# Unit 2's attention in two query chunks, with the first MoE product of batch 0 begun beside the second chunk

## The chip, the cores and the metric

One core of a Trainium2 chip runs the whole kernel. The metric is the time on the device, in microseconds (us), as the median of several runs. A core has five engines that run their own instruction streams, each in program order, and wait for each other through semaphores: TensorE (PE: matrix products into the accumulators in PSUM), VectorE (DVE), ScalarE (ACT: exponentials and other functions), GpSimd (POOL) and SyncE (SP, which issues transfers). DMA engines move data between the memory of the chip and the core's own memory.

## The reference

```python
def _attn_ref(q, k, v, g_q, g_k):                      # q, k, v: (8, 12, 448, 64)
    def rmsnorm(x, g):
        rms = np.sqrt(np.mean(x * x, axis=-1, keepdims=True) + 1e-06)
        return x / rms * g
    q_n, k_n = (rmsnorm(q, g_q), rmsnorm(k, g_k))
    scores = scale * np.matmul(q_n, k_n.transpose(0, 1, 3, 2))
    scores = scores - np.max(scores, axis=-1, keepdims=True)
    attn = np.exp(scores)
    attn = attn / (np.sum(attn, axis=-1, keepdims=True) + 1e-09)
    return np.matmul(attn, v).astype(np.float32)

def _moe_ref(x, w_in, w_out):                          # x: (3584, 768)
    h = x @ w_in                                       # w_in: (768, 2048)
    g = np.maximum(0.01 * h, h)
    return (g @ w_out).astype(np.float32)              # w_out: (2048, 768)
```

Attention with normalised queries and keys, and behind it two products with a leaky ReLU between them. A token of the second part is one position of one batch, and its 768 features are the 12 heads, so the first product of a batch needs the attention of all its heads, for those tokens that it is to compute.

## The kernel before

The work is cut into 24 **units** of four heads; three units make a batch. A unit's path is:

1. load the queries and keys (DMA), square them (ACT or POOL), sum the squares (DVE), form 1/rms by a logarithm and an exponential (ACT, `prep_rinv`), multiply (DVE, `prep_norm`), transpose (PE, `prep_tr`) and copy out of PSUM (DVE or ACT);
2. scores of the first of seven key tiles, their maximum over everything (DVE, `shift_max`), which a product with a matrix of ones spreads to all partitions (`shift_mm`); this is what the exponentials subtract, one number for the whole unit;
3. for each of the seven key tiles the scores (PE, `qk`) and their exponential (ACT, `ex`);
4. the row sums (PE, `zsum`), their reciprocal by logarithm and exponential (ACT, `zinv`), the product with the values (PE, `pv`), and that times the reciprocal (DVE, `xmul`), which gives `xt`, the input of the first MoE product.

The 448 positions of a head lie as seven groups of 64. PSUM has eight banks: two slots of two banks (`slot()`) and four single banks (`aux()`), which come from a pool or, after `hold()`, from a list that `drop()` fills.

```python
    def aux(shape, dtype, name):
        if held:
            return held[0].pop(0)
        return psum.tile(shape, dtype, tag="aux", bufs=4, name=name)

    def hold():
        if not held:
            banks = [psum.tile([P, 512], FP32, tag="aux", bufs=4, name=f"bank{i}") for i in range(4)]
            held.append(banks)

    def drop(bank):
        if held:
            held[0].append(bank)
    ...
    def prep_rinv(u, tis=BOTH):
        x = slice(tis[0], tis[-1] + 1)
        nc.scalar.activation(buf(u, "uu")[:, x], buf(u, "ssq")[:, x], AF.Ln, bias=eps_t, scale=1.0 / D)
        nc.scalar.activation(buf(u, "rinv")[:, x], buf(u, "uu")[:, x], AF.Exp, bias=0.0, scale=-0.5)
    ...
    def prep_tr(u, ti, copies):
        tp = aux([P, NS, P], FP16, "tp")
        for (lo, hi), copy in copies:
            for x in range(lo, hi):
                nc.tensor.transpose(tp[:, x, :], buf(u, "n16")[:, ti, x].rearrange("p a d -> p (a d)"), ident16)
            copy(buf(u, "qkT")[:, ti, lo:hi], tp[:, lo:hi], ti == 0)
    ...
    def slot():
        return psum.tile([P, 2, 512], FP32, tag="sT", bufs=2, name="sT")
    ...
    def score(u, t, banks):
        for r in range(2):
            for a in range(2):
                nc.tensor.matmul(banks[a][64 * r:64 * r + 64, 0:S].rearrange("p (t x) -> p t x", t=NS),
                                 kT(u, r, a, t), qT(u, r, a), start=True, stop=True)
    ...
    def ex(u):
        s = st[u]
        ...
        for t, sT in s["sT"]:
            if isinstance(sT, list):
                for a in range(2):
                    nc.scalar.activation(s["et"][:, t, a], sT[a][:, 0:S], AF.Exp, bias=s["eb"], scale=1.0)
            else:
                nc.scalar.activation(s["et"][:, t], sT[:, :, 0:S], AF.Exp, bias=s["eb"], scale=1.0)

    def score0(u):
        banks = [aux([P, 512], FP32, "s0") for a in range(2)]
        score(u, 0, banks)
        st[u]["sT"] = [(0, banks)]

    def shift_max(u):
        s = st[u]
        sT = s["sT"][0][1]
        if isinstance(sT, list):
            pm2 = small.tile([P, 2], FP32, tag="pm2", name="pm2")
            for a in range(2):
                nc.vector.tensor_reduce(pm2[:, a:a + 1], sT[a][:, 0:S], axis=AXL.X, op=ALU.max)
            s["spare"] = sT[0]
            nc.vector.tensor_reduce(s["spare"][:, 511:512], pm2, axis=AXL.X, op=ALU.max)
        else:
            s["spare"] = sT[:, 0]
            nc.vector.tensor_reduce(s["spare"][:, 511:512], sT[:, :, 0:S], axis=AXL.XY, op=ALU.max)
        s["dg"] = small.tile([P, P], FP16, tag="dg", name="dg")
        nc.vector.tensor_tensor(s["dg"], ident16, s["spare"][:, 511:512].broadcast_to([P, P]), op=ALU.mult)
    ...
    def zsum(u, t0=0, t1=NS):
        s = st[u]
        for t in range(t0, t1):
            for r in range(2):
                for a in range(2):
                    nc.tensor.matmul(s["zt"][r][64 * a:64 * a + 64, 0:S], ones16[64 * r:64 * r + 64],
                                     s["et"][64 * r:64 * r + 64, t, a], start=(t == 0), stop=(t == NS - 1))
    ...
    def pv(u, t0=0, t1=NS):
        s = st[u]
        if t0 == 0 and "pslot" not in s:
            s["pv"] = [aux([P, 512], FP32, "pv") for r in range(2)]
        for t in range(t0, t1):
            for r in range(2):
                for a in range(2):
                    nc.tensor.matmul(s["pv"][r][64 * a:64 * a + 64, 0:S], vts[u % NV][64 * r:64 * r + 64, a, t],
                                     s["et"][64 * r:64 * r + 64, t, a], start=(t == 0), stop=(t == NS - 1))

    def xmul(u):
        s = st[u]
        b, g = divmod(u, NQ)
        if b not in xts:
            xts[b] = xpool.tile([P, NQ, 2, S], FP16, tag="xt", name="xt")
        for r in range(2):
            nc.vector.tensor_tensor(xts[b][:, g, r], s["pv"][r][:, 0:S], s["rz"][:, r], op=ALU.mult)
            drop(s["pv"][r])

    def prelu(b, dst, src):
        if b % 2 == 0:
            src = src.rearrange("p (t x) -> p t x", t=NS)[:, ::-1]
            dst = dst.rearrange("p (t x) -> p t x", t=NS)
        nc.scalar.activation(dst, src, AF.Prelu, bias=0.0, scale=1.0, alpha=0.01)

    def moe1(b, ft):
        xt = xts[b]
        hps = aux([P, 512], FP32, "hps")
        for kt in range(KT):
            nc.tensor.matmul(hps[:, 0:S], win16[:, kt // 2, kt % 2, ts(ft, P)], xt[:, kt // 2, kt % 2],
                             start=(kt == 0), stop=(kt == KT - 1))
        prelu(b, gt[:, ft, 64 * (b % 2):64 * (b % 2) + S], hps[:, 0:S])
        drop(hps)
```

`moe1` is one of 16 tiles of the first MoE product of a batch: six matmuls over all 448 tokens, and a leaky ReLU on ACT into `gt`; `moe1_part` does some of the six matmuls of the first two tiles, and `sums` is `zsum` and `pv` for some key tiles. `zinv` stands in the diff below. MoE items stand in a queue, and from unit 3 on `fill` puts some of them between the steps of the attention, so many that the queue lasts until the next batch is finished. The order in which everything is issued is fixed by the program. From the middle of unit 1 on, and the start of the loop (the part before it is in the diff):

```python
        trn(2, 1, vcopy)
        xmul(0)
        qk(1, (4,))
        ex(1)
        qk(1, (5,))
        ex(1)
        score0(2)
        shift_max(2)
        qk(1, (6,))
        ex(1)
        shift_bank(2)
        warm(12, st[2]["pb"])
        shift_mm(2)
        prep_ssq(3)
        ex(2)
        qk(2, (1,))
        ex(2)
        zsum_slot(1)
        pv(1)
        prep_rinv(3)
        zinv(1)

        prep_norm(3)
        ...
        qk(2, (2,))
        ex(2)
        trn(3, 0, vcopy)
        trn(3, 1, vcopy)
        xmul(1)
        prep_ssq(4)
        qk(2, (3,))
        ex(2)
        qk(2, (4,))
        ex(2)
        st[2]["zt"] = [aux([P, 512], FP32, "zt") for r in range(2)]
        sums(2, 0, 3)
        qk(2, (5,))
        ex(2)
        sums(2, 3, 4)
        qk(2, (6,))
        ex(2)
        prep_rinv(4)
        sums(2, 4, 5)
        qk(3, STEPS[0])
        sums(2, 5, NS)
        zinv(2)
        shift_max(3)
        xmul(2)
        push(0)
        first = slot()
        moe1_part(0, first, 0, KT - 2)
        shift_mm(3)
        ex(3)
        moe1_part(0, first, KT - 2, KT - 1)
        moe1_part(0, first, KT - 1, KT)
        for ft in range(2):
            prelu(0, gt[:, ft, 0:S], first[:, ft, 0:S])
        del queue[0:2]

        for u in range(3, NU):
            for d in range(4):
                if d > 0 or u > 3:
                    qk(u, STEPS[d])
                    if d == 0:
                        shift_max(u)
                        if u == 6:
                            xmul_sb(u - 2)
                        if narrow(u - 1):
                            pv_slot(u - 1)
                            zcol(u - 1)
                            shift_mm(u)
                            pv_out(u - 1)
                        else:
                            zsum_slot(u - 1)
                            pv(u - 1)
                            shift_mm(u)
                            zinv(u - 1)
                    ex(u)
                ...
                if d == 0:
                    if u == 3:
                        prep_norm(4)
                        gate(4)
                    ...
                if (u, d) in ((3, 1), (4, 0)):
                    for ti in range(2):
                        prep_tr(u + 1, ti, VV)
                ...
                fill(u, d, jobs)
```

`warm` issues products that nobody reads.

## Time and profile before

| what | value |
|---|---|
| median of three runs | 421.74 us (421.12 to 422.13) |
| span of the profiled execution | 420.3 us |
| PE busy | 404.4 us (96%), 3959 matmuls |
| ACT busy | 303.6 us (72%) |
| DVE busy | 269.2 us (64%) |
| POOL busy | 83.0 us (20%) |
| moved by DMA | 62.42 MB |

The page of the profile gives the busy time of each engine, then the span in 40 slices of 10.5 us, each a digit for the busy share in tenths. Matmuls are pipelined, so a busy PE is not PE at its peak. The timeline lists instructions by time, with like ones merged: start, duration, engine, line of the program, operation, what is written and read, the shapes, the count, and in brackets how long the engine stood idle before and what ended that. The table by stages gives busy times for stretches of the span. The chain of waits follows the last instruction back through what released each step.

### The profile page before, as it was taken

How to read it: one execution, taken by the hardware profiler on the slowest of the kernel's cores; microseconds unless marked ns; L12 is line 12 of the kernel's file. 1: busy time of each engine (PE TensorE's matmuls, PEld its weight loads, DVE VectorE, ACT ScalarE, POOL GpSimd, SP SyncE). 2: the span in 40 equal slices, each digit the busy share in tenths (PEclk: the TensorE clock that was granted, in tenths of full speed). 3: DMA queues.
4: the chain of work that ended last, by engine and by line, in shares of the span. 5: the costliest groups of instructions: out<-in, count | busy, mean ns of one | idle time of the engine just before them, and what ended most of it. 6: DMA issues, size and time to landing. Idle time of an engine off the chain costs nothing.

```text
span 420.3 us, 9568 instructions
## 1 busy us (share of the span) xinstructions
PE 404.4 (96%) x3959; PEld 222.9 (53%) x3959; DVE 269.2 (64%) x440; ACT 303.6 (72%) x474; POOL 83.0 (20%) x75
## 2 busy tenths in 40 slices
PE   7977999999999999999999999999999999999995
PEld 6544444555445544555445544455445557558853
DVE  5788665787658736466448745467338787527762
ACT  5999878868987689867986779967986657653600
POOL 1958422300020111210121111120101101010000
PEclk9699999999999999999999999999999999999999
DMA  8999999889664795678565796578562460032023
GB/s 257 218 239 237 235 250 147 200 156 215 169 153 68 224 212 120 168 163 180 152 130 107 194 203 150 151 141 170 180 111 44 121 155 11 7 78 75 2 53 100
DMA packets 71951, 62.42 MB, mean 149 GB/s; under 512 B 36324, under 2 KB 67044, under 8 KB 71908
## 3 DMA queue, kind: packets, MB, share of 16 engines
q1 hardware_dynamic: 61312, 49.62, 47.2%
q0 software_dynamic: 10272, 11.80, 18.1%
q8 instruction: 31, 0.51, 0.5%
q10 hardware_dynamic: 324, 0.39, 0.3%
q14 instruction: 12, 0.10, 0.1%
HBM read 45.61 MB, written 11.01 MB: 135 GB/s over the span
## 4 chain that ended last, share of the span: by engine, by line
PE 83%; ACT 8%; DVE 6%; issue 1%; DMA 1%; SPq 0%; DVEq 0%; ACTq 0%
PE hps L362 27%; PE sT L195 8%; PE sT L340 6%; PE ma L444 5%; PE md L444 5%; PE mc L444 5%; ACT et L214 5%; PE bank L444 5%; PE bank L564 4%; PE op L403 3%; PE zc L283 3%; PE mb L444 3%; DVE n L167 2%; PE sT L444 2%; PE bank L403 1%
## 5 line engine op out<-in xcount | busy, mean ns | idle before, releaser
L214 ACT ACTIVATE et<-sT,eb 128x896 f16<-128x896 f32 x166 | 159.4, 1010 | 18.6 <-PE sT L195 16.9
L362 PE MATMUL hps<-xt,win 128*128 128x448 f16 x600 | 120.8, 353 | 0.2 <-DVE xt L349 0.2
L362 PEld LDWEIGHTS <-win 128*128 128x128 f16 x612 | 56.8, 98 | 58.2 <-issue 9.6
L320 POOL TENSOR_TENSOR xt<-x,rz 128x896 f16<-128x896 f32 x16 | 33.4, 2085 | 148.0 <-DMA rz<-zs 139.5
L356 ACT ACTIVATE gt<-hps 128x448 f16<-128x448 f32 x100 | 54.0, 556 | 6.1 <-PE hps L362 5.4
L167 DVE TENSOR_TENSOR n<-rq,rinv 128x896 f16<-128x896 f32 (+2 forms) x25 | 27.2, 1090 | 47.0 <-ACT rinv L161 44.2
L195 PE MATMUL sT<-qkT 64*64 64x448 f16 x664 | 53.2, 369 | 3.0 <-ACT et L214 1.9
L155 DVE TENSOR_REDUCE ssq<-sq 128x14 f32<-128x896 f32 (+2 forms) x49 | 50.3, 1058 | 1.6 <-ACT sq L144 1.6
L444 PEld LDWEIGHTS <-sa 128*128 128x128 f16 x352 | 32.8, 98 | 26.3 <-issue 6.1
L295 ACT COPY x<-sT 128x896 f32<-128x896 f32 x19 | 17.2, 906 | 36.4 <-DVE sT L245 36.4
L124 POOL DMA_DIRECT2D vt<-in_v_dram x24 | 18.2, 757 | 114.9 <-PE sT L340 107.4
L444 PEld LDWEIGHTS <-gt 128*128 128x128 f16 x264 | 25.2, 98 | 18.7 <-issue 2.1
L195 PEld LDWEIGHTS <-qkT 64*64 64x64 f16 x672 | 15.2, 105 | 36.8 <-issue 33.5
L340 PE MATMUL sT<-et,vt 64*64 64x448 f16 x532 | 28.5, 350 | 0.3
L403 PE MATMUL op<-wout,gt 128*128 128x384 f16 x160 | 28.4, 327 | 0.0
L232 DVE TENSOR_REDUCE sT<-sT 128x1 f32<-128x896 f32 x22 | 24.1, 1093 | 4.3 <-PE sT L195 4.3
L340 PEld LDWEIGHTS <-vt 64*64 64x64 f16 x672 | 20.7, 107 | 11.3 <-issue 1.7
L167 DVE TENSOR_TENSOR n<-rk,rinv 128x896 f16<-128x896 f32 (+2 forms) x26 | 26.1, 1009 | 0.0
L403 PEld LDWEIGHTS <-gt 128*128 128x128 f16 x192 | 17.6, 98 | 14.3 <-issue 3.0
L444 PE MATMUL ma<-wout,gt 128*128 128x384 f16 x128 | 23.5, 326 | 0.0
L425 DVE TENSOR_TENSOR sa<-gt 128x512 f16<-128x512 f16 (+1 forms) x15 | 8.2, 544 | 18.5 <-ACT gt L356 13.9
L144 ACT ACTIVATE sq<-rq 128x896 f32<-128x896 f32 (+2 forms) x18 | 16.3, 913 | 1.3 <-DMA rq<-in_q_dram 1.3
(135 smaller groups left out, 516.6 us busy)
## 6 DMA issues: line engine op xcount, KB each, us to landing
rq<-in_q_dram SPq DMA_DIRECT2D x24, 448.0 KB, 3.9
rk<-in_k_dram SPq DMA_DIRECT2D x24, 448.0 KB, 5.6
out_dram<-ost SPq DMA_DIRECT2D x52, 192.0 KB, 3.3
rz<-zs SPq DMA_DIRECT2D x76, 112.0 KB, 2.3
vt<-in_v_dram POOLq DMA_DIRECT2D x24, 224.0 KB, 5.1
win<-in_moe_w_in_dram POOLq DMA_DIRECT2D x8, 384.0 KB, 16.8
wout<-in_moe_w_out_dram POOLq DMA_DIRECT2D x2, 1536.0 KB, 29.7
out_dram<-ost SPq DMA_DIRECT2D x4, 96.0 KB, 2.1
```

Source lines behind the costliest of these rows:

```text
L124: nc.gpsimd.dma_start(vts[u % NV].rearrange("p a t d -> p a (t d)"), rows(v, u))
L155: nc.vector.tensor_reduce(buf(u, "ssq")[:, ti, :, c[0]:c[1]], buf(u, f"sq{ti}")[:, :, c[0]:c[1]], axis=AXL.X, op=ALU.add)
L167: nc.vector.tensor_tensor(buf(u, "n16")[:, ti, c[0]:c[1]].rearrange("p s a d -> p a s d"), src[:, :, c[0]:c[1]], buf(u, "rinv")[:, ti, :, ...
L195: nc.tensor.matmul(banks[a][64 * r:64 * r + 64, 0:S].rearrange("p (t x) -> p t x", t=NS), kT(u, r, a, t), qT(u, r, a), start=True, stop=True)
L214: nc.scalar.activation(s["et"][:, t], sT[:, :, 0:S], AF.Exp, bias=s["eb"], scale=1.0)
L232: nc.vector.tensor_reduce(s["spare"][:, 511:512], sT[:, :, 0:S], axis=AXL.XY, op=ALU.max)
L320: eng.tensor_tensor(xts[b][:, g], s["x32"], s["rz"], op=ALU.mult)
L340: nc.tensor.matmul(s["pv"][r][64 * a:64 * a + 64, 0:S], vts[u % NV][64 * r:64 * r + 64, a, t], s["et"][64 * r:64 * r + 64, t, a], start=(t ...
L356: nc.scalar.activation(dst, src, AF.Prelu, bias=0.0, scale=1.0, alpha=0.01)
L362: nc.tensor.matmul(hps[:, 0:S], win16[:, kt // 2, kt % 2, ts(ft, P)], xt[:, kt // 2, kt % 2], start=(kt == 0), stop=(kt == KT - 1))
L403: nc.tensor.matmul(op2[:, 0:HC], gt[:, ft, ds(col(t), P)], wout16[:, ft, ds(HC * half, HC)], start=(ft == 0), stop=(ft == FT - 1))
L444: nc.tensor.matmul(bank[:, 0:HC], a[:, f], b[:, f], start=(first and f == 0), stop=(f == HF - 1), skip_group_check=not first)
```

## The change

The first three units form batch 0, and until they are done there is no MoE work to put between the steps. The change makes such work available earlier. Unit 2 is attended in two chunks of its queries, groups 0 to 3 (256 of 448, `QA`) and groups 4 to 6 (192, `QB`): scores, exponentials, row sums, product with the values and reciprocal are done for the first chunk over all seven key tiles, and then for the second. When the first chunk is through, the first MoE product of batch 0 can begin on those tokens, and stands in the program between the second chunk's steps. So the first product of batch 0 goes in the same two token chunks, two tiles at a time in one bank (`moe1_two`): 96 matmuls of 256 columns and 96 of 192 in place of 96 of 448. Scores of two key tiles share a slot, so one exponential covers two of them.

With it come changes of order and place in the prelude: the four single banks are held in a list from the start of the program to the end of unit 2; unit 1's transposed queries are copied by DVE in place of ACT, and its keys 1 to 6 after the maximum in place of before; unit 0's two products with the reciprocal are split, one of them behind the maximum of unit 2; unit 2's scores for the maximum are issued before two of unit 1's steps and are computed again for the exponential; unit 3's transposes come later; some counts of `warm` differ. Everything from unit 3 on has the same program but for the queue's items.

```diff
@@ -68,6 +68,7 @@
+    hold()
...
+    def tp_bank():
+        bank = aux([P, 512], FP32, "tp")
+        return bank, bank.bitcast(FP16)[:, 0:NS * P].rearrange("p (s x) -> p s x", s=NS)
...
+    def score_c(u, steps, c):
+        n = 64 * (c[1] - c[0])
+        sT = slot()
+        for i, t in enumerate(steps):
+            for r in range(2):
+                for a in range(2):
+                    nc.tensor.matmul(sT[64 * r:64 * r + 64, a, n * i:n * i + n].rearrange("p (t x) -> p t x", x=64),
+                                     kT(u, r, a, t), qT(u, r, a)[:, c[0]:c[1]], start=True, stop=True)
+        st[u]["sT"] = (steps, sT)
+
+    def ex_c(u, c):
+        s = st[u]
+        n = 64 * (c[1] - c[0])
+        if "et" not in s:
+            s["et"] = epool.tile([P, NS, 2, S], FP16, tag="et", name="et")
+        steps, sT = s["sT"]
+        m = len(steps)
+        nc.scalar.activation(s["et"][:, steps[0]:steps[0] + m, :, 64 * c[0]:64 * c[1]].rearrange("p m a n -> p a m n"),
+                             sT[:, :, 0:n * m].rearrange("p a (m n) -> p a m n", n=n), AF.Exp, bias=s["eb"], scale=1.0)
 
...
-    def zinv(u):
+    def zinv(u, x=ALLQ):
         s = st[u]
         s["rz"] = zpool.tile([P, 2, S], FP32, tag="rz", name="rz")
         if "zslot" in s:
-            nc.scalar.activation(s["rz"], s["zslot"][:, :, 0:S], AF.Ln)
-            nc.scalar.activation(s["rz"], s["rz"], AF.Exp, bias=0.0, scale=-1.0)
+            nc.scalar.activation(s["rz"][:, :, x], s["zslot"][:, :, x], AF.Ln)
+            nc.scalar.activation(s["rz"][:, :, x], s["rz"][:, :, x], AF.Exp, bias=0.0, scale=-1.0)
         else:
             for r in range(2):
-                nc.scalar.activation(s["rz"][:, r], s["zt"][r][:, 0:S], AF.Ln)
-                nc.scalar.activation(s["rz"][:, r], s["rz"][:, r], AF.Exp, bias=0.0, scale=-1.0)
-
...
+    def xmul(u, rs=(0, 1), x=ALLQ):
         s = st[u]
         b, g = divmod(u, NQ)
         if b not in xts:
             xts[b] = xpool.tile([P, NQ, 2, S], FP16, tag="xt", name="xt")
-        for r in range(2):
-            nc.vector.tensor_tensor(xts[b][:, g, r], s["pv"][r][:, 0:S], s["rz"][:, r], op=ALU.mult)
+        for r in rs:
+            nc.vector.tensor_tensor(xts[b][:, g, r, x], s["pv"][r][:, x], s["rz"][:, r, x], op=ALU.mult)
             drop(s["pv"][r])
 
...
+    def moe1_two(b, f, c, k0=0, k1=KT, bank=None):
+        n = 64 * (c[1] - c[0])
+        if bank is None:
+            bank = aux([P, 512], FP32, "hps")
+        for i in range(2):
+            for kt in range(k0, k1):
+                nc.tensor.matmul(bank[:, n * i:n * i + n], win16[:, kt // 2, kt % 2, ts(f + i, P)], xts[b][:, kt // 2, kt % 2, cut(c)],
+                                 start=(i == 0 and kt == 0), stop=(kt == KT - 1), skip_group_check=True)
+        if k1 == KT:
+            src = bank[:, 0:2 * n].rearrange("p (f t x) -> p f t x", f=2, x=64)[:, :, ::-1]
+            dst = gt[:, f:f + 2, 64 * (NS - c[1]):64 * (NS - c[0])].rearrange("p f (t x) -> p f t x", x=64)
+            nc.scalar.activation(dst, src, AF.Prelu, bias=0.0, scale=1.0, alpha=0.01)
+            drop(bank)
+        return bank
 
...
+    QA, QB = (0, 4), (4, NS)
...
+        if b == 0:
+            items = [(w, lambda f=f, c=c: (flush(), moe1_two(b, f, c))) for w, c in ((1.28, QA), (0.96, QB)) for f in range(0, FT, 2)]
...
-        warm(8, wb)
+        warm(6, wb)
+        drop(wb)
         qk(0, (3,))
-        tr(1, 0, ((ALL, acopy),))
-        tpk = tr(1, 1, ((K0, vcopy),))
+        tr(1, 0, ((ALL, vcopy),))
+        tpk = tr(1, 1, ((K0, vcopy),), None, False)
         ex(0)
         qk(0, (4,))
         ex(0)
-        tr(1, 1, ((K1, vcopy),), tpk)
         score0(1)
         shift_max(1)
         shift_bank(1)
-        warm(10, st[1]["pb"])
         qk(0, (5,))
         ex(0)
+        tr(1, 1, ((K1, None),), tpk, False)
         warm(8, st[1]["pb"])
         qk(0, (6,))
         ex(0)
+        warm(10, st[1]["pb"])
         shift_mm(1)
+        vcopy(buf(1, "qkT")[:, 1, 1:NS], tpk[1][:, 1:NS])
+        drop(tpk[0])
         prep_ssq(2)
         ex(1)
         qk(1, (1,))
@@ -862,67 +921,80 @@
         qk(1, (3,))
         ex(1)
         trn(2, 1, vcopy)
-        xmul(0)
+        xmul(0, (0,))
         qk(1, (4,))
-        ex(1)
-        qk(1, (5,))
         ex(1)
         score0(2)
         shift_max(2)
+        qk(1, (5,))
+        ex(1)
         qk(1, (6,))
         ex(1)
         shift_bank(2)
-        warm(12, st[2]["pb"])
+        warm(8, st[2]["pb"])
         shift_mm(2)
+        for a in range(2):
+            drop(st[2]["sT"][0][1][a])
+        xmul(0, (1,))
         prep_ssq(3)
-        ex(2)
-        qk(2, (1,))
-        ex(2)
+        score_c(2, (0, 1), QA)
+        ex_c(2, QA)
+        score_c(2, (2, 3), QA)
+        ex_c(2, QA)
         zsum_slot(1)
         pv(1)
         prep_rinv(3)
         zinv(1)
-
         prep_norm(3)
         load(6)
         gate(3)
         prep_sqp(4, (1,))
         prep_sqp(5)
         load_v(5)
-        qk(2, (2,))
-        ex(2)
+        score_c(2, (4, 5), QA)
+        ex_c(2, QA)
+        xmul(1)
+        st[2]["zt"] = [aux([P, 512], FP32, "zt") for r in range(2)]
+        zsum(2, 0, 4, cut(QA))
+        score_c(2, (6,), QA)
+        ex_c(2, QA)
+        zsum(2, 4, NS, cut(QA))
+        pv(2, 0, NS, cut(QA))
+        zinv(2, cut(QA))
+        score_c(2, (0, 1), QB)
+        ex_c(2, QB)
+        xmul(2, (0, 1), cut(QA))
+        first = [moe1_two(0, 2 * i, QA, 0, KT - 2) for i in range(2)]
+        score_c(2, (2, 3), QB)
+        ex_c(2, QB)
         trn(3, 0, vcopy)
+        moe1_two(0, 0, QA, KT - 2, KT, first[0])
         trn(3, 1, vcopy)
-        xmul(1)
         prep_ssq(4)
-        qk(2, (3,))
-        ex(2)
-        qk(2, (4,))
-        ex(2)
-        st[2]["zt"] = [aux([P, 512], FP32, "zt") for r in range(2)]
-        sums(2, 0, 3)
-        qk(2, (5,))
-        ex(2)
-        sums(2, 3, 4)
-        qk(2, (6,))
-        ex(2)
+        moe1_two(0, 2, QA, KT - 2, KT, first[1])
+        push(0)
+        del queue[0:2]
+
+        def mo(n):
+            for x in range(n):
+                queue.pop(0)[1]()
+
+        score_c(2, (4, 5), QB)
+        ex_c(2, QB)
+        mo(1)
+        score_c(2, (6,), QB)
+        ex_c(2, QB)
+        qk(3, STEPS[0])
+        shift_max(3)
+        mo(1)
+        zsum_slot(2, cut(QB))
+        pv(2, 0, NS, cut(QB))
         prep_rinv(4)
-        sums(2, 4, 5)
-        qk(3, STEPS[0])
-        sums(2, 5, NS)
-        zinv(2)
-        shift_max(3)
-        xmul(2)
-        push(0)
-        first = slot()
-        moe1_part(0, first, 0, KT - 2)
         shift_mm(3)
         ex(3)
-        moe1_part(0, first, KT - 2, KT - 1)
-        moe1_part(0, first, KT - 1, KT)
-        for ft in range(2):
-            prelu(0, gt[:, ft, 0:S], first[:, ft, 0:S])
-        del queue[0:2]
+        zinv(2, cut(QB))
+        xmul(2, (0, 1), cut(QB))
+        held.clear()
 
         for u in range(3, NU):
             for d in range(4):

```

## The prediction, made before the changed kernel had run

> **What bounds the kernel now.** I began with the page's row of slices, to see where TensorE (PE) is not full, and went from there to the table by stages, the timeline of each engine, and the chain of waits.
>
> ```profile
> PE   7977999999999999999999999999999999999995
> ACT  5999878868987689867986779967986657653600
> ```
>
> PE is full from the fifth slice (42 us) to the last but one: there the MoE products fill every gap of the attention. In the first four slices it is not, and ACT is the busier engine. The change touches units 0 to 2, so only the stretch up to some 49 us can give anything, and later work is moved, not removed. The table by stages (columns: length, then busy us and count of PE, its weight loads, DVE, ACT, POOL, then clock, DMA) sizes it:
>
> ```profile
> 34.00:38.00 4.00, 2.57 (x36) 1.46 (x37) 3.93 (x6) 3.54 (x5) 2.90 (x5) 1.00 1.11 247
> 38.00:41.90 3.90, 3.27 (x57) 1.67 (x53) 3.29 (x4) 3.38 (x6) 3.79 (x3) 1.00 1.15 236
> 41.90:44.94 3.04, 2.54 (x18) 1.24 (x15) 1.98 (x7) 1.89 (x5) 0.09 (x1) 1.00 1.17 234
> 44.94:48.60 3.66, 3.66 (x36) 2.02 (x35) 2.16 (x3) 3.50 (x6) 1.21 (x3) 1.00 1.18 216
> ```
>
> From 44.94 on PE is continuous. The PE timeline shows what it did until then (start, duration, matmuls; in brackets the idle time and who ended it):
>
> ```profile
> 30.44 0.22 PE L250 MATMUL pb<-dg,onesp 128*128 128x128 f16 x1 [0.41 <-DVE dg L234]
> 30.59 0.38 PE L195 MATMUL sT<-qkT 64*64 64x448 f16 x4
> 30.80 1.49 PE L265 MATMUL sT<-et,ones 64*64 64x448 f16 x28
> 32.12 1.49 PE L340 MATMUL pv<-et,vt 64*64 64x448 f16 x28
> 33.45 0.36 PE L195 MATMUL sT<-qkT 64*64 64x448 f16 x4
> 34.96 0.56 PE L175 MATMUL tp<-ident,n 128*128 128x128 f16 x7 [1.16 <-DVE n L167]
> ...
> 44.56 0.54 PE L370 MATMUL sT<-xt,win 128*128 128x448 f16 x2 [0.50 <-DVE xt L349]
> 44.94 2.43 PE L362 MATMUL hps<-xt,win 128*128 128x448 f16 x12
> 47.30 0.57 PE L195 MATMUL sT<-qkT 64*64 64x448 f16 x8
> 47.80 0.95 PE L175 MATMUL tp<-ident,n 128*128 128x128 f16 x14
> ```
>
> Durations include the drain of the last matmul, so I count starts. A row sum of 28 takes 32.12 - 30.80 = 1.32 us, so a set of four scores 0.19; seven transposes about 0.4; one 448-wide MoE matmul 0.19. From 30.44 to 44.94 PE then did seven score sets (1.33), two row sums and two attn x V (5.3), 14 transposes (0.8), twelve MoE matmuls (2.28) and one broadcast (0.1): 9.8 us of work in 14.5. **About 4.7 us of PE time is lost here**, and that is the most the change can win. Who takes it, on ACT and DVE:
>
> ```profile
> 31.22 1.16 ACT L212 ACTIVATE et<-s,eb 128x448 f16<-128x448 f32 x2 [0.61 <-DVE eb L253]
> 33.69 0.90 ACT L326 ACTIVATE rz<-sT 128x896 f32<-128x896 f32 x1
> 44.94 1.01 ACT L214 ACTIVATE et<-sT,eb 128x896 f16<-128x896 f32 x1 [1.09 <-DVE eb L253]
> 44.82 1.08 DVE L167 TENSOR_TENSOR n<-rq,rinv 128x896 f16<-128x896 f32 x1
> 45.82 1.08 DVE L167 TENSOR_TENSOR n<-rk,rinv 128x896 f16<-128x896 f32 x1
> ```
>
> The chain of waits runs through these: exponentials, DVE's normalisation of the next unit, its copies and the product with 1/z. The last two rows matter later: unit 4 is normalised by 46.9, before PE asks for it at 47.80.
>
> **What the Trainium skill says.** "TensorE: Matmul & The Clock Gate", Back-to-back issue gap: a matmul costs its columns at the full clock plus about 2.5 ns, so cutting 448 columns into 256 and 192 adds one such floor. The trace agrees: twelve 128-wide warm matmuls begin within (0.84 - 0.22)/11 = 56 ns of each other. "TensorEngine Tiling (Array Packing)", Key Properties: changing the tiling mode drains the engine. The trace agrees: between MoE items eight 64x64 scores run from 62.89 to 63.40, 0.51 us where two sets are 0.38, and the twelve MoE matmuls after them take 2.37 where 12 x 0.19 is 2.28, so a round trip costs some 0.22 us. "ScalarE: Activation LUTs", What ACT_TABLE_LOAD costs: an ACTIVATE is a fixed cost plus 0.833 ns an element. Here 896 elements follow each other at 0.895 us and 448 at 0.525, so 0.155 + 0.826 ns each. "PSUM — Partial Sum Buffer", Engine vs sequencer instructions: the VectorE queue is strictly first in, first out; every DVE row here stands in program order.
>
> **The change, part by part.** *Exponentials of unit 2.* Before: five of 896 and two halves, 6 x 0.895 + 1.05 = 6.4. After: first chunk three of 1024 (1.0 each) and one of 512 (0.58), second three of 768 (0.79) and one of 384 (0.47): 6.4. Nothing won on ACT. The Ln/Exp of 1/z are 1.3 + 0.95 against 2.2, the activations of a pair of MoE tiles 0.58 + 0.47 against 1.1: equal too.
>
> *The start of units 1 and 2.* Unit 1's queries are copied by DVE, not ACT (1.01 us at 17.33 goes), and its key copy moves behind the maximum. Exponentials of unit 1 start some 0.6 earlier, but that copy (0.56) now stands ahead of DVE's sums of squares for unit 2, which before begin at 21.48 and decide when unit 2 is normalised. I expect that at 24.4 as before: **0 won**. For unit 2 one of two products (0.57) goes behind the maximum: its exponentials begin at about 30.75 for 31.22, 0.45 earlier. But ACT then waits for the sums of squares of unit 3, which end at 33.2 as before.
>
> *Chunk by chunk.* From there by hand: 1/z of unit 1 ends at 35.7, the third and fourth exponentials of the first chunk at 36.6 and 37.2, its row sums at 37.5, its attn x V at 38.1, its 1/z at 38.8, the products at 39.5. PE idles from 35.3 to 36.7, but at 38.3 takes up the sixteen first-product matmuls that need units 0 and 1 only, and is continuous after that: 16 x 0.109 = 1.75, four score pieces 0.33, transposes 0.8, the eight closing matmuls 0.87, two more pairs 2 x 1.31, second row sums and attn x V 2 x 0.56, unit 3's first scores 0.19. Without mode changes this ends at 46.1, with 4 x 1.31 = 5.2 us of MoE done; before, the same point without MoE is 44.94 - 2.28 = 42.7, now 46.1 - 5.2 = 40.9. **Won: 1.7 to 1.8 us.**
>
> *What it adds.* Three more round trips of the tiling mode, 3 x 0.22 = 0.65. Chunked MoE of batch 0: 96 more matmuls x 2.5 ns = 0.24 less what I counted in the 1.31, so 0.15. Unit 2's scores of its first key tile twice: counted.
>
> *What it moves.* Unit 3's first exponential waits for its maximum, after the second attn x V: at about 47.5 for 44.94. On ACT the second 1/z stands behind it (0.9 + 0.95), then DVE's two products (0.5), and only then, in DVE's order, the normalisation of unit 4 (2.1). That gives 50.0 to 52.1 instead of 44.8 to 46.9. PE meanwhile has two filler items (2.6) and two score sets, is at unit 4's transposes at about 50.2, and waits: for the queries until 51.1, for the keys until 52.1 less 0.4 of work: **lost: 1.4 us**. Against this, later in unit 3 nothing more: with 2.9 us less filler in the queue until unit 6, PE waits a little longer for ACT's slots (0.37 before at 53.46), but ACT comes less far behind. I put +0.2.
>
> Sum: -1.75 + 0.65 + 0.15 + 1.4 + 0.2 = +0.65. I put all waits in series, and a few tenths of them will overlap, so I take **+0.1: 421.8 us**.
>
> **Rivals.** *A: the gap is filled and nothing comes back.* Unit 4's transposes would not wait, because unit 3's shift comes sooner than I think. For it: ACT is busy 11.8 of the 14.5 us from 30.4 to 44.9, and PE's filler is elastic. Against: the DVE order above. Time: 421.74 - 1.75 + 0.8 = 420.8, or 420.0 if the mode changes are hidden in waits. *B: the weights are late.* First-product columns 1024 and up come in four loads; the last was issued at 23.10 and landed 23.0 us later, at 46.1. The chunked order reaches these columns at about 47.0, 0.9 after. If contention delays them by 2 us, PE stands for 1: 422.8. DMA is busy at 1.1 to 1.2 of its share throughout, which speaks for it; that no load moves earlier speaks against. *C: PSUM banks.* After the hand-over from the held banks to the pool, the first filler item could get a bank that the last products (50.0) still read: 3 us lost, 424.5. Against: in the profile before, the row sums at 36.86 take banks freed earlier by the transposes, so banks come in the order of release. *D: the clock.* PE stands for 1.4 us in one piece; before it stood 1.16 at 33.8 and the clock stayed at 1.00. A half clock for one stretch would cost up to 3 us; unlikely.
>
> **Range and chances.** A gives 420.0 to 420.8, my sum 422.4, B 422.8, C and D 424 and up. Eight in ten: 420.0 to 423.4. The whole stake, 4.7 us, is 1.1% of the time, so over 2% either way needs something I don't see: faster 0.01, same 0.98, slower 0.01.
>
> **What would show it.** Right: PE busy from about 38.3 without a hole to the shift of unit 3; DVE's normalisation of unit 2 still near 24.4; that of unit 4 near 50; PE waiting over 1 us in sum for it at the transposes of unit 4; MoE items beginning some 6 us earlier. Wrong: transposes of unit 4 without a wait (then A), or a wait on the weights or a bank at 47 (B, C), or a clock under 1.00 after 20 us.

## The result, and the profile after

The changed kernel takes **428.62 us** (median of four runs, 426.91 to 429.44) against 421.71 us (also four, 421.12 to 422.13): ratio 1.016, interval 1.0126 to 1.0193. The prediction had 421.8 us and a range to 423.4.

The slices of the page, after:

```profile
PE   7877899988999999999999999999999999999996
ACT  5888778656996679967986788967986748653600
```

PE's first, third and fourth slices are at 7 as before, the second and fifth have 8 for 9, and the ninth and tenth (85 to 107 us) have 8 where the kernel before had 9: the loss reaches far behind the part that was edited. The table by stages (columns as before) shows the early part as the change meant it:

```profile
34.00:38.00 4.00, 2.90 (x76) 2.23 (x69) 3.36 (x5) 3.64 (x6) 2.87 (x5) 1.00 1.12 260
38.00:42.00 4.00, 3.83 (x78) 3.04 (x71) 0.82 (x3) 2.60 (x6) 2.60 (x2) 1.00 1.16 245
42.00:46.00 4.00, 4.00 (x52) 2.96 (x49) 3.64 (x5) 3.44 (x6) 1.27 (x1) 1.00 1.14 261
46.00:50.00 4.00, 4.00 (x83) 3.40 (x82) 1.50 (x4) 2.25 (x6) 1.11 (x2) 1.00 1.16 212
```

PE is full from 38.3 us on, up to unit 4's transposes, and not only from 45. The PE timeline of the changed kernel over the same part:

```profile
33.01 1.52 PE L298 MATMUL sT<-et,ones 64*64 64x448 f16 x28 [0.88 <-ACT et L240]
37.72 0.41 PE L298 MATMUL bank<-et,ones 64*64 64x256 f16 x8 [1.10 <-ACT et L240]
...
39.46 1.92 PE L407 MATMUL bank<-xt,win 128*128 128x256 f16 x16
...
48.16 0.23 PE L277 MATMUL bank<-dg,onesp 128*128 128x128 f16 x1
48.23 2.78 PE L407 MATMUL hps<-xt,win 128*128 128x256 f16 x24
50.94 0.57 PE L201 MATMUL sT<-qkT 64*64 64x448 f16 x8
52.67 0.56 PE L180 MATMUL tp<-ident,n 128*128 128x128 f16 x7 [1.16 <-DVE n L168]
53.67 0.56 PE L180 MATMUL tp<-ident,n 128*128 128x128 f16 x7 [0.44 <-DVE n L168]
```

The first product begins at 39.46 for 41.94. PE still stands ahead of it, 0.88 us at 33.01 and 1.10 at 37.72, both times for ACT's exponentials. And unit 4's transposes wait 1.60 us in sum for DVE. ACT and DVE there:

```profile
31.84 2.12 ACT L240 ACTIVATE et<-sT,eb 128x1024 f16<-128x1024 f32 x2 [0.18 <-DVE eb L281]
...
49.02 1.01 ACT L221 ACTIVATE et<-sT,eb 128x896 f16<-128x896 f32 x1 [0.97 <-DVE eb L281]
51.00 0.62 DVE L383 TENSOR_TENSOR xt<-bank,rz 128x192 f16<-128x192 f32 x2 [2.01 <-ACT rz L360]
51.54 1.08 DVE L168 TENSOR_TENSOR n<-rq,rinv 128x896 f16<-128x896 f32 x1
52.53 1.08 DVE L168 TENSOR_TENSOR n<-rk,rinv 128x896 f16<-128x896 f32 x1
```

DVE stands 2.01 us for unit 2's second reciprocal before it may normalise unit 4, which it could have done meanwhile: ACT had unit 4's 1/rms ready at 48.05.

**Where the time went.** A good ruler is the moment at which a unit's shift is ready on DVE. Between two shifts I take the elapsed time from both profiles, and from it the PE time of the MoE items (from one matmul's start to the next, waits left out, each matmul in the stretch in which it begins), so that work which only moved does not count:

| stretch | elapsed before | elapsed after | MoE before | MoE after | net, after less before |
|---|---|---|---|---|---|
| start to unit 2's shift | 31.03 | 31.59 | 0 | 0 | +0.56 |
| to unit 3's | 13.72 | 17.24 | 2.25 | 6.30 | -0.53 |
| to unit 4's | 14.97 | 15.32 | 8.53 | 6.96 | +1.92 |
| to unit 5's | 14.27 | 13.78 | 9.01 | 8.37 | +0.15 |
| to unit 6's | 13.13 | 13.70 | 8.69 | 7.46 | +1.80 |
| to unit 7's | 13.42 | 14.96 | 8.77 | 8.94 | +1.37 |
| to the end | 319.77 | 320.21 | | | +0.44 |

The nets make 5.7; with 0.8 more MoE time in all (38.03 against 37.25) that is the 6.5 between the spans, 426.8 and 420.3. So the early start, for which the change was made, is worth half a microsecond, and the 0.8 us of additional MoE time stand against it. PE's idle time between the shifts of units 2 and 3 shows why it is so little: 2.75 us before and still 2.28 after. The first row is +0.75 up to unit 1's shift (22.16 for 21.41), where the clock differs between the two profiles, and -0.19 from there to unit 2's (9.43 for 9.62), at full clock in both. Three later stretches lose far more: that to unit 4's shift, with the transposes that I had foreseen, and those to unit 6's and unit 7's (called units 5 and 6 below), which I had not. In the table by stages of the two kernels the last two look so, first before, then after:

```profile
73.98:87.11 13.13, 13.03 (x139) 6.87 (x138) 10.95 (x15) 8.48 (x12) 3.92 (x3) 1.00 0.87 191
87.11:100.53 13.42, 13.06 (x138) 6.70 (x136) 10.42 (x15) 10.57 (x15) 0.71 (x1) 1.00 0.97 197
```

```profile
77.93:91.63 13.70, 12.02 (x131) 6.37 (x130) 11.04 (x15) 8.60 (x12) 3.91 (x3) 1.00 0.80 183
91.63:106.59 14.96, 13.22 (x138) 6.70 (x136) 10.51 (x15) 10.71 (x15) 0.72 (x1) 1.00 0.84 186
```

Unit 5's stretch has eight matmuls fewer and takes longer; PE stands for 1.68 and 1.74 us in the two, where before it stood for 0.10 and 0.36.

### The profile page after: what moved, and what is told of

Its sections match the earlier page's. It is cut to its first block, busy times and chain, and to the rows that moved or that the text cites. A ratio compares the mean times of both kernels' runs of the same rounds, so it can differ in the third digit from the quotient of the medians.

```text
span 426.8 us, 9931 instructions
## 1 busy us (share of the span) xinstructions
PE 406.5 (95%) x4137; PEld 233.0 (55%) x4137; DVE 269.5 (63%) x443; ACT 303.7 (71%) x474; POOL 83.0 (19%) x75
## 4 chain that ended last, share of the span: by engine, by line
PE 81%; DVE 9%; ACT 7%; issue 1%; DMA 1%; SPq 0%; DVEq 0%
PE hps L396 23%; PE sT L201 8%; PE sT L374 6%; PE ma L493 5%; PE md L493 5%; PE bank L493 5%; PE mc L493 5%; PE bank L614 4%; ACT et L221 4%; PE op L452 4%; PE zc L316 3%; DVE n L168 3%; PE mb L493 3%; DVE ssq L156 2%; PE sT L493 2%; PE hps L407 1%
## 5 line engine op out<-in xcount | busy, mean ns | idle before, releaser
L221 ACT ACTIVATE et<-sT,eb 128x896 f16<-128x896 f32 x160 | 154.0, 1011 | 19.0 <-PE sT L201 17.4
L396 PE MATMUL hps<-xt,win 128*128 128x448 f16 x516 | 103.7, 353 | 1.6 <-DVE xt L353 1.6
L396 PEld LDWEIGHTS <-win 128*128 128x128 f16 x528 | 49.1, 98 | 51.7 <-issue 10.1
L168 DVE TENSOR_TENSOR n<-rq,rinv 128x896 f16<-128x896 f32 (+2 forms) x25 | 26.2, 1052 | 50.3 <-ACT rinv L162 48.2
L201 PE MATMUL sT<-qkT 64*64 64x448 f16 x640 | 51.1, 371 | 3.3 <-DVE qkT L780 1.8
L390 ACT ACTIVATE gt<-hps 128x448 f16<-128x448 f32 x86 | 46.6, 559 | 4.6 <-PE hps L396 4.1
L201 PEld LDWEIGHTS <-qkT 64*64 64x64 f16 x648 | 14.2, 105 | 35.2 <-issue 29.3
L407 PEld LDWEIGHTS <-win 128*128 128x128 f16 x192 | 16.6, 98 | 3.1 <-issue 1.5
```

The costliest lines, as they stand in the source:

```text
L168: nc.vector.tensor_tensor(buf(u, "n16")[:, ti, c[0]:c[1]].rearrange("p s a d -> p a s d"), src[:, :, c[0]:c[1]], buf(u, "rinv")[:, ti, :, ...
L407: nc.tensor.matmul(bank[:, n * i:n * i + n], win16[:, kt // 2, kt % 2, ts(f + i, P)], xts[b][:, kt // 2, kt % 2, cut(c)], start=(i == 0 an ...
```

## The experiments

Four theories. **A**: unit 4's normalisation is late because it stands on DVE behind unit 2's last products. **A2**: the shorter queue puts its items into other steps of units 5 and 6, and PE waits there; later sharpened to **A3**, which names what waits. **B**: the chunks themselves cost PE time. **C**: the half clock lasts longer. That is a stretch near the start in which PE is granted half of its clock; the pages show it in the second slice (10.5 to 21 us), first before, then after:

```profile
PEclk9699999999999999999999999999999999999999
PEclk9599999999999999999999999999999999999999
```

It lasts 6.8 us in the profile before and 10.2 us in that after. It also differs between executions of one program: the changed kernel and four of the experiments (unit 4's normalisation first, the fixed places, the sums first, both mended) are the same up to unit 3's shift, and their profiles have 10.2, 10.2, 0, 10.2 and 3.4 us of it, with unit 1's shift at 22.16, 22.47, 20.17, 22.20 and 20.20. So medians of a few runs carry 1 us or more of chance (a lower mean clock, the average over an execution, marks the longer half clock); stretches of single profiles in which the clock is 1.00 do not.

### Unit 4's normalisation first

```diff
         shift_mm(3)
+        prep_norm(4)
         ex(3)
         zinv(2, cut(QB))
...
-                        prep_norm(4)
                         gate(4)
```

> The changed kernel with unit 4's normalisation issued ahead of unit 2's last two products on DVE. Theory A (lost order: PE stands 1.16 + 0.44 us at unit 4's transposes because that normalisation is queued behind those products): the wait at the transposes goes, unit 4's shift comes 1.5 us earlier, and the time falls by about 1.5 us against the changed kernel, to some 427.0; less if the later waits of units 5 and 6 swallow it. Theory B (the chunked products themselves cost PE time) and theory C (the longer half clock): no change beyond 0.3 us.

Measured: 425.07 us (424.83 to 428.04), ratio to the kernel before 1.0086 (1.0062 to 1.011). The PE timeline of this run at the transposes:

```profile
52.30 0.57 PE L201 MATMUL sT<-qkT 64*64 64x448 f16 x8
52.80 0.96 PE L180 MATMUL tp<-ident,n 128*128 128x128 f16 x14
```

Fourteen transposes in one piece, no wait. The stretch from unit 3's shift to unit 4's is 13.48 us for 15.32, **1.84 shorter**, and the stretches of units 5 and 6 are as in the changed kernel (13.71 and 14.95). A holds. The medians are 3.55 apart, more than the 1.84: one of these six executions has a mean clock of 0.988, but three of the four of the changed kernel. At 0.99 or more it is 424.91 for 426.91. Unit 2's products, which now stand behind, start at 52.35, and nothing waits for them.

### Second-product items where they were

```diff
+    PLAN = {(3, 0): 2, (3, 1): 1, (3, 2): 1, (3, 3): 2, (4, 0): 1, (4, 1): 2, (4, 2): 1, (4, 3): 2,
+            (5, 0): 2, (5, 1): 1, (5, 2): 1, (5, 3): 2, (6, 0): 2, (6, 1): 1, (6, 2): 2}
...
-        while queue and debt[0] >= queue[0][0] * 0.5:
+        n = PLAN.get((u, d))
+        while queue and (debt[0] >= queue[0][0] * 0.5 if n is None else n > 0):
...
+            n = None if n is None else n - 1
```

> The changed kernel with the queue's items placed by a fixed list: the twelve items of the second product stand in the same steps of units 5 and 6 as in the kernel before, and the chunked first product is spread up to the last step of unit 4. Theory A2 (the shorter queue puts too few or the wrong items into units 5 and 6, and PE waits there): the idle time of 1.7 us each in units 5 and 6 falls to under 0.5, some of it comes back in units 3 and 4, net 1.5 to 3 us faster than the changed kernel, 425.6 to 427.1. Theory B and theory C: no change beyond 0.5 us.

Measured: 426.59 us (426.1 to 428.89), ratio 1.0124 (1.01 to 1.0148). From unit 4's shift to unit 7's it takes 12.40 + 13.12 + 14.56 = 40.1 us against 42.4 in the changed kernel, with idle PE time of 0.10 and 0.36 in the last two for 1.68 and 1.74. (Unit 6's 14.56 hold six matmuls of batch 1 more, 1.1 us.) So A2 holds for that part. But from unit 7's shift to the end it takes longer than any other kernel here (columns as above):

```profile
102.23:424.50 322.27, 313.99 (x2935) 171.86 (x2932) 197.03 (x321) 224.59 (x355) 43.08 (x29) 1.00 0.55 125
```

That is 2.1 us more than the changed kernel's 320.21. I had fixed the places but left the queue's running account as the fixed places happened to leave it, so the items of later batches fell elsewhere, and PE waits anew (0.45 at 132.05 for ACT, 0.51 at 134.87 and 0.98 at 182.90 for DVE; 4.06 in all, where the changed kernel waits 1.14). It is a second instance of the same effect, by accident. That the median lies in the range expected is luck: from unit 2's shift to the end this profile is only 0.3 us shorter than the changed kernel's (394.9 for 395.2), and the rest of the 2.0 between the medians comes from ahead of that, where the clock differs.

### Twelve unread products for six

```diff
-        warm(6, wb)
+        warm(12, wb)
```

> The changed kernel with twelve unread products in place of six at one place in unit 0, where the changed kernel had taken two out. Theory C (the half clock lasts 10.2 us in place of 6.8 because PE is less busy in the third of its windows): the full clock is back by about 18.1 us, unit 1's shift comes 0.7 us or more earlier, and the time falls by 0.8 to 1.6. Theories A and A2: this is at most 0.8 of the 6.9 us lost.

Measured: 427.68 us (426.75 to 429.47), ratio 1.0142 (1.0117 to 1.0167). Two of five executions still had a mean clock of 0.988, as three of four of the changed kernel. These products do not decide it. At a mean clock of 0.99 or more this kernel takes 426.75 to 427.68 and the changed kernel's one such execution 426.91, so **about 1.7 us of the 6.9 are the clock's**, and over 5 are not. Its profile says the same: it has no half clock at all near the start, unit 2's shift comes 1.56 us earlier (30.03), and from there every stretch to unit 7's shift is that of the changed kernel to 0.01 us.

### The chunks alone

```diff
+        if b == 0:
+            items = items[0:2] + [(w, lambda f=f, c=c: (flush(), moe1_two(b, f, c))) for w, c in ((1.28, QA), (0.96, QB)) for f in range(2, FT, 2)]
```

with `moe1_two` and `cut` as in the change, all else as before.

> The kernel before with only the first product of batch 0 (tiles 2 to 15) in two token chunks, all of it still behind unit 2. Theory B (96 more matmuls and their mode changes): 0.5 to 0.8 us slower than before by PE work alone. If the chunking carried the whole loss it would be 5 us or more slower. Theories A, A2, C: not over 1 us slower.

Measured: 422.0 us (421.16 to 423.54), ratio 1.0007 (0.9995 to 1.0018). B falls as a cause of the large loss: the first product in two chunks costs at most 0.8 us, and the medians say 0.3. Unit 2's attention is undivided in this run, so what its chunks cost is not in these figures. The items have the new costs here too, and some of the second product move (o4 and o10 below, each by one step), but none of its copies ahead of the sums of squares that the next section is about: PE's idle time in units 5 and 6 is 0.20 and 0.22.

### The sums of squares ahead of the items

Which wait is it in units 5 and 6? The account of the queue, worked through for both kernels, gives these items in each step (o0 to o11 are halves of the second product of batch 0, and behind each odd one DVE copies a finished half of the output):

| unit, step | before | changed |
|---|---|---|
| 4, 3 | two of the first product | o0 |
| 5, 0 | o0 o1 | o1 o2 |
| 5, 1 | o2 | **o3** |
| 5, 2 | o3 | o4 |
| 5, 3 | o4 o5 | o5 |
| 6, 0 | o6 o7 | o6 o7 |
| 6, 1 | o8 | **o8 o9** |
| 6, 2 | o9 o10 | o10 |

In step 1 DVE also sums the squares of the unit after next. In the changed kernel the copy of o3 falls ahead of these sums, and that of o9 a unit later. The DVE timeline before, from 3.97 us behind unit 5's shift on, and that of the changed kernel, where the sums begin 5.01 us behind it:

```profile
77.95 2.07 DVE L155 TENSOR_REDUCE ssq<-sq 128x14 f32<-128x896 f32 x2
79.94 1.66 DVE L419 TENSOR_TENSOR tw<-wout,tw 128x1536 f16<-128x1536 f16 x1
81.53 0.55 DVE L407 COPY ost<-op 128x384 f32<-128x384 f32 x1
```

```profile
82.10 0.56 DVE L456 COPY ost<-op 128x384 f32<-128x384 f32 x1 [1.79 <-PE op L452]
82.58 0.45 DVE L152 TENSOR_SCALAR qkT<-qkT,gcol 128x896 f16<-128x896 f16 x1
82.94 2.07 DVE L156 TENSOR_REDUCE ssq<-sq 128x14 f32<-128x896 f32 x2
```

DVE stands 1.79 us in front of a copy whose matmuls are not done, with the sums behind it. What follows on ACT and PE:

```profile
85.04 0.32 ACT L161 ACTIVATE uu<-ssq,eps_t 128x28 f32<-128x28 f32 x1 [0.71 <-DVE ssq L156]
86.57 0.38 PE L201 MATMUL sT<-qkT 64*64 64x448 f16 x4 [0.39 <-ACT et L221]
87.47 1.52 PE L374 MATMUL sT<-et,vt 64*64 64x448 f16 x28 [0.52 <-ACT et L221]
90.44 0.22 PE L271 MATMUL sT<-dg,onesp 128*128 128x64 f16 x2 [0.67 <-DVE dg L261]
...
96.96 1.91 ACT L221 ACTIVATE et<-sT,eb 128x896 f16<-128x896 f32 x2 [1.04 <-PE sT L201]
...
103.10 0.54 PE L396 MATMUL hps<-xt,win 128*128 128x448 f16 x2 [1.64 <-DVE xt L353]
```

ACT's logarithm waits 0.71, its exponentials behind it are late, PE waits for them twice, and the shift behind that; the last two lines are unit 6's. The experiment moves the sums, and the scaling of queries (L152) that stands ahead of them, and nothing else (they are the first three of the step's jobs):

```diff
+        if (u, d) in ((5, 1), (6, 1)):
+            for job in jobs[0:3]:
+                job()
+            del jobs[0:3]
```

> The changed kernel with one thing else: in the second steps of units 5 and 6 the unit-7 and unit-8 sums of squares (and the scaling of unit 6's and 7's queries) are issued before the queue's items, so that they do not stand behind an output copy on DVE. The queue's items stay where they are, just as many and in the same steps. Theory A3 (not the shortness of the queue, but an output copy of a second-product item that now falls ahead of the sums of squares in DVE's order, and waits there for PE): PE's idle time in units 5 and 6 falls from 1.7 us each to under 0.7, and the time by 1.5 to 2.5 us against the changed kernel, to about 424.5 to 425.5 at the same clock. If the shortness of the queue alone makes PE wait, the idle time stays above 1.4 in each and the time within 0.5 us.

Measured: 426.46 us (424.54 to 427.94), ratio 1.0099 (1.0071 to 1.0127); four of its six executions had a mean clock of 0.987 or 0.988, the other two took 424.54 and 424.66. DVE and PE in this run:

```profile
80.30 0.45 DVE L152 TENSOR_SCALAR qkT<-qkT,gcol 128x896 f16<-128x896 f16 x1
80.66 2.07 DVE L156 TENSOR_REDUCE ssq<-sq 128x14 f32<-128x896 f32 x2
82.65 0.55 DVE L456 COPY ost<-op 128x384 f32<-128x384 f32 x1
```

```profile
86.17 0.38 PE L201 MATMUL sT<-qkT 64*64 64x448 f16 x4
86.71 1.52 PE L374 MATMUL sT<-et,vt 64*64 64x448 f16 x28 [0.16 <-ACT et L221]
...
94.92 0.57 PE L201 MATMUL sT<-qkT 64*64 64x448 f16 x8
...
100.91 0.54 PE L396 MATMUL hps<-xt,win 128*128 128x448 f16 x2 [1.05 <-DVE xt L353]
```

Unit 5's stretch is 12.04 us for 13.70, its idle PE time 0.26 for 1.68: with the same items in the same steps, so **A3 holds and shortness alone is refuted there**. Unit 6's is 14.37 for 14.96 with 1.15 idle; 1.05 is left in front of the first item of batch 1, more than the 0.7 I expected. There A3 is not the whole cause. With o8 and o9 both in step 1, the scores of step 2 begin at 94.92, 4.88 us behind the shift (3.59 before). ACT stands 1.04 us for them, as in the changed kernel, its logarithm comes behind their exponentials, and DVE's normalisation waits 0.84 us for that. The two stretches together are 2.2 us shorter, as theory A3 had it.

### Both mended, and the account set back

Unit 4's normalisation and the fixed places as above, and with them:

```diff
+        if (u, d) == (6, 2):
+            debt[0] = -0.64
```

> The changed kernel with unit 4's normalisation ahead of unit 2's last products, with the fixed placing of the queue's items, and with the queue's account set at the end of the first stretch to what it is in the kernel before, so that all later items fall as they did before. Theory A + A2: 1.8 us from the first and 2.4 to 3.0 from the second and third against the changed kernel: 423.5 to 424.5, and the stretch from unit 7's shift to the end as long as in the kernel before (319.8 us) within 0.4. Theory B or C: above 426.

Measured: 422.29 us (420.79 to 425.09), ratio 1.0011 (0.9995 to 1.0027). The table by stages for units 5, 6 and the rest:

```profile
72.77:85.90 13.13, 13.03 (x139) 6.87 (x138) 10.95 (x15) 8.49 (x12) 3.91 (x3) 1.00 0.86 195
85.90:99.33 13.43, 13.07 (x138) 6.70 (x136) 10.43 (x16) 10.58 (x16) 0.71 (x1) 1.00 0.81 179
```

```profile
99.33:419.00 319.67, 314.47 (x2941) 172.24 (x2938) 194.50 (x321) 225.26 (x356) 43.10 (x29) 1.00 0.56 127
```

The first two are the stretches of the kernel before to a hundredth, and the third is 0.10 shorter. 6.3 of the 6.9 us are back by the medians. Without the start and its clock, from unit 2's shift to unit 7's, it is 69.69 us, for 69.50 before and 75.00 in the changed kernel: 5.3 of 5.5. It came out somewhat better than expected.

### Fewer changes of the tiling mode

```diff
         score_c(2, (0, 1), QB)
         ex_c(2, QB)
+        score_c(2, (2, 3), QB)
+        ex_c(2, QB)
         xmul(2, (0, 1), cut(QA))
         first = [moe1_two(0, 2 * i, QA, 0, KT - 2) for i in range(2)]
-        score_c(2, (2, 3), QB)
-        ex_c(2, QB)
         trn(3, 0, vcopy)
-        moe1_two(0, 0, QA, KT - 2, KT, first[0])
         trn(3, 1, vcopy)
-        prep_ssq(4)
+        moe1_two(0, 0, QA, KT - 2, KT, first[0])
         moe1_two(0, 2, QA, KT - 2, KT, first[1])
+        prep_ssq(4)
```

> As the run before it, with unit 2's scores for the second chunk's key tiles 2 and 3 issued ahead of the first MoE pieces, and unit 3's transposes together, so that PE changes its tiling mode one round trip less often and ACT does not wait 0.9 us for those scores. Prediction from the chunk stage: 1.06 us above the pure matmul time is spent there on mode changes; one round trip of 0.2 to 0.3 goes, and the exponentials come 0.9 us sooner, which the end of the stage, PE-bound, does not feel: 0.2 to 0.5 us faster than that run. Theory C: no change.

Measured: 421.27 us (420.66 to 424.12), ratio 0.9996 (0.9979 to 1.0013). The stretch to unit 3's shift is 17.01 us for 17.24: 0.23, the lower end of what was expected. PE's idle time in it is 2.28 in both, so the 0.23 lie in PE's work, where the round trip is what was taken out; the prediction had put 0.22 for one. The 1.06 us of the expectation were misread: they come from 48 matmuls of 0.109 us against 6.30, but 54 begin in that stretch, six of them of the queue's first item, and their 5.89 leave 0.41. The medians are 1.0 apart, more than the 0.23; among the executions with a mean clock of 0.99 or more they are so too (421.05 for 422.01), so the clock does not explain the rest, and it stays open.

### Unit 1 as before

The part of the change in unit 1 is put back in the changed kernel (copies by ACT, keys ahead of the maximum, unread products as they were):

```diff
-        warm(6, wb)
+        warm(8, wb)
...
-        tr(1, 0, ((ALL, vcopy),))
+        tr(1, 0, ((ALL, acopy),))
...
+        tr(1, 1, ((K1, vcopy),), tpk)
         score0(1)
```

> The changed kernel with only unit 1's part put back as it was (queries copied by ACT, keys 1 to 6 copied ahead of the maximum, the unread products in the old places and numbers). Theory C (the half clock lasts three windows, 10.2 us, because of this part): no execution has a mean clock under 0.99, unit 1's shift comes at 20.5 to 21.5 in each, and the median falls from 428.6 to about 427.0. Theory A (order in units 4 to 6) leaves it there, over 5 us slower than the kernel before. If the half clock comes from elsewhere, some executions stay at 0.988.

Measured: 427.08 us (426.67 to 428.5), ratio 1.0134 (1.0117 to 1.0152). The median fell as C said, and unit 1's shift came at 21.20 in the profile, but one of four executions still had 0.988, so C's attribution to unit 1's part is **not shown**: four executions against four cannot tell it. A is not touched: over 5 us are still lost.

### All mended

Unit 1 as before, together with the run with fewer changes of mode (both diffs above).

> The run with fewer switches of the tiling mode, with unit 1's part put back as it was. All that was found is mended in it: theory A, A2 and C together expect 420.5 to 421.2, that is 0.5 to 1.2 us faster than the kernel before, since the early start of the first product wins about 0.75 us up to unit 3's shift, and the chunks cost 0.3. If the unit-1 part was of use for more than the clock, it is no faster than 421.3.

Measured: 421.26 us (420.41 to 422.4), ratio 0.9991 (0.998 to 1.0002). That is just outside the 420.5 to 421.2 expected, and the interval does not tell it from the kernel before. In its profile the clock is at one half from 30.9 to 34.3 us, in unit 2, where PE waits 0.89 us for a slot, and three of 14 executions had 0.988. The stretch from unit 2's shift to unit 3's is 18.13 us there for 17.01 in the run with fewer changes of mode, with the same program in it and the clock at 1.00. In the changed kernel PE waits 0.88 us at the same place and the clock stays at 1.00, so the wait alone does not bring the half clock. The next run adds unread products:

```diff
-        warm(8, st[2]["pb"])
+        warm(12, st[2]["pb"])
...
         ex_c(2, QA)
+        wb = aux([P, 512], FP32, "warm")
+        warm(14, wb)
+        drop(wb)
         zsum_slot(1)
```

> The run with all mended, with eighteen more unread products in unit 2 (four ahead of its shift, fourteen in the 0.9 us in which PE waits for a slot ahead of unit 1's row sums, a stretch in which that run's profile shows the clock at one half from 30.9 to 34.3 us). If the half clock there comes of PE's waits and costs time, no execution falls to a mean clock of 0.988, and the median falls by 0.2 to 0.5 us, to about 420.8 to 421.1, clear of the kernel before. If it costs nothing there, or is not moved by these products, the time stays at 421.2 to 421.5.

Measured: **421.01 us** (420.36 to 421.99), ratio **0.9981 (0.9973 to 0.9989)**: faster than the kernel before by 0.8 us, and than the changed kernel by 7.6. None of 19 executions fell below 0.989. Whether the unread products did that or chance is not told apart: the step from the run before it, 0.25 us, is smaller than its spread. Nor is the 0.8 us the early product's. In this profile, as in that before, the clock is at 1.00 from unit 1's shift on. From there to unit 2's it takes 9.11 us for 9.62, and from unit 2's to unit 7's 69.45 for 69.50. The half microsecond lies in the new order ahead of unit 2's shift; the chunks and the early product, all told, are worth nothing that these profiles show.

## Why the prediction was wrong, point by point

- *Equal work on ACT, a small surcharge on PE*: right. ACT is busy 303.7 us for 303.6. The MoE matmuls take 0.78 us more of PE up to unit 7's shift, for which 0.65 + 0.15 had been put; the chunks alone cost 0.3 us of the kernel's. (The sum for unit 2's exponentials before is right with its six of 896; the word "five" beside it is a slip.)
- *Nothing won in unit 1, 0.45 in unit 2*: from unit 1's shift to unit 2's 0.19 came of the 0.45. DVE's normalisation of unit 2 began at 25.42 for 24.37 and not near 24.4: 0.75 of that is unit 1's shift, which comes later with 10.2 us of half clock for 6.8, and 0.30 lies behind the shift, where the copy of the keys (0.55 us) now stands ahead of the sums of squares, as foreseen.
- *1.7 to 1.8 won up to unit 3's shift*: **0.53 measured**, with the surcharge left out of both. Right in kind, a third in size. The prediction took all of the time above the pure matmul times, 4.7 us, for what could be won; but PE is busy in part of it, and the rows of its own table have only 2.6 us of idle PE from 34 to 44.94. It also saw one hole in the changed kernel, 1.4 us from 35.3, where PE stood 0.88 at 33.01 and 1.10 at 37.72. MoE began 2.5 us earlier and not "some 6": the profile before has its first MoE matmuls at 41.94, and 44.94 is only the queue's first item.
- *Unit 4's transposes wait 1.4 us*: right. They waited 1.60, the stretch lost 1.92, and issuing the normalisation first brought back 1.84.
- *"Against this, later in unit 3 nothing more: with 2.9 us less filler in the queue until unit 6, PE waits a little longer for ACT's slots ... I put +0.2"*: **this is the step that failed.** Units 5 and 6 lost 1.80 and 1.37. I treated the queue as a quantity of filler; it is also an order. The shorter queue moved the second product's items by one step: in both units an output copy came ahead of the sums of squares in DVE's order, and in unit 6 two items came ahead of the scores of step 2. Moving only the sums took 1.66 from unit 5's stretch and 0.59 from unit 6's, and placing the items as before took both losses away.
- *A few tenths will overlap, so +0.1 and not +0.65*: wrong in direction; the table shows no such overlap.
- *Rivals.* A did not occur, since the transposes waited. B (late weights) and C (banks) did not occur: the last columns landed 18.3 us after their issue at 22.40, at 40.7, and the queue's first item, at 48.23, followed the shift's product at 48.16 without a wait. D (the clock) did occur, but before 22 us and not where I looked: about 1.7 us by the medians, 0.75 between the two profiles.

Term by term, measured for predicted: the early start -0.53 for -1.75, the surcharge +0.78 for +0.80, unit 4's transposes +1.92 for +1.4, the later stretches of units 5 and 6 +3.17 for +0.2, and, where nothing had been put, +0.56 up to unit 2's shift, +0.15 in unit 4 and +0.44 in the later batches. That is +6.5 for +0.65. The 2.97 of the fourth term are half of the difference.

## What to carry to other kernels

Work that is dealt out by a running account lands elsewhere when its total changes. After such a change compare each engine's order step by step in the stages that were *not* touched, above all where a copy out of PSUM stands ahead of something that another chain needs. A copy that is issued right behind its matmuls makes everything behind it on its engine wait for PE, 1.79 us here: issue the work that is ready first. A stage's gain is to be reckoned without the work it only moved: four microseconds of earlier products were half a microsecond of time, and they made 0.8 us of additional matmul time. And of the time above the pure matmul times (4.7 us here) only the idle part (2.6) can be filled with other matmuls.

## What the runs showed of the hardware that was not expected

- The half clock at the start is not a constant of a kernel. Its stretches lasted 3.4, 6.8 or 10.2 us in the profiles here, that is one, two or three times 3.41 us (the "windows" of the expectations), or did not occur at all, and one fell at 30.9 us. Executions of the changed kernel at a mean clock of 0.988 took 428.5 to 429.4 us, the one at 0.998 took 426.9.
- In the run with unit 4's normalisation moved, the half clock lasted from 16.6 to 26.9 us and that execution took 428.04; its five others, at 0.994 to 1.000, took 424.8 to 425.8.
- One round trip of PE's tiling mode between 128x128 and 64x64 cost 0.23 us, when one was taken out and the idle time of the stretch stayed at 2.28 us.
